# Sums on GpSimd that wait for VectorE's token mix, a cast moved to ScalarE, and wider token mixes of odd batches

## The chip, the core and the metric

The kernel runs on one core of one Trainium2 chip. The metric is the device time of one execution in microseconds, as the median of several executions. The core's engines are TensorE (PE, with its weight loads as PEld), VectorE (DVE), ScalarE (ACT), GpSimd (POOL) and SyncE (SP, which issues most of the DMAs). Each engine takes its own instructions in the order in which the kernel writes them; between engines, semaphores hold an instruction back until its data are there.

## What is computed

Eight batches, each with 8 heads, 576 tokens and a head size of 64. Keys and values are averaged over groups of 8 tokens, so every query meets 72 keys. The attention's result is then the input x (576 x 512 per batch) of a residual MLP block with a token mix:

```python
k_p = k.reshape(B, H, Sp, pool, D).mean(axis=3)          # pool = 8, Sp = 72
v_p = v.reshape(B, H, Sp, pool, D).mean(axis=3)
attn = softmax(scale * q @ k_p.T)                        # per head
x = (attn @ v_p).transpose(0, 2, 1, 3).reshape(B, S, H * D)
tok = np.einsum('ts,bsd->btd', w_tok, alpha1 * x + beta1)
u = x + lam * tok
ch = np.maximum((alpha2 * u + beta2) @ w_ch1, 0.0) @ w_ch2
out = u + lam * ch
```

All inputs and the output are float32; the kernel multiplies in bfloat16 and float16.

## The kernel before

**Blocks.** The tokens are cut into 36 chunks of 128: four per batch, and one more for each pair of batches that holds the last 64 tokens of both. Nine blocks (loop over `n`, L698) take four chunks each through the MLP: 16 first-layer tiles `mlp_A` (four matmuls each into `ps_h`, then a Relu on ScalarE, L547, into `Hj`) and four times four groups `mlp_B` (four matmuls each into `ps_ch`, L565). Beside them, block n carries the attention and the token mix of batch n+1 (`attention(b)`, L665, with b = n+1), so that blocks 0 to 6 do both and blocks 7 and 8 the MLP alone. Batch 0 is done ahead of the loop.

**The order.** Every engine's order is written out by hand. In each block a list `todo` collects pairs of a position and a step; the list is sorted by position (equal ones stay as appended) and carried out in that order (L731). `mlp_A(j)` stands at j, 0 to 15, and the groups of `mlp_B` at 16 to 31; the attention's steps get positions between these. A negative position stands at the head of the block. The order decides only what is ahead of what on each engine; an engine that has nothing to wait for runs ahead into the next block.

**The steps that matter here**, in the order of a batch, with the engine and the line:
- `cast_rem` (L117): the last 64 tokens of q cast, of k summed; GpSimd, three instructions (L121, L123, L124).
- `cast_q` (L128): one half of the heads' q, 128 x 1024 float32, to bfloat16 (L130). GpSimd, for batches 2 to 7.
- `sum_k` (L133): k summed over groups of 8 in three adds (L138 twice, L139), the last into `k_bf`; GpSimd.
- `sum_v_rem` (L430, GpSimd, into `vrem`) and `sum_v` (L411, VectorE, L415 twice and L417, into `v_sum`): the same for v.
- `att_F`, `att_Frem` (L361, L376): transposes of q on TensorE, copied into `qT` by ScalarE (L372, L389).
- `att_K` (L392): TensorE brings the sums of k into `kpT`, copied by VectorE (L407); it also reads `rem_k`.
- `att_V`, `att_Vrem` (L420, L436): the same for v into `vp1`, copied by ScalarE (L427, L443).
- `att_S` (L445): scores of a head in two halves, with an exp on ScalarE each (L454). `att_AV` (L456): five matmuls, then VectorE normalizes into `x` (L474, L476).
- `att_X` (L479): x times lam*alpha1, per pair of heads, into `xs`, the token mix's input; GpSimd for the first three pairs, VectorE for the last.
- `mix_T` (L503): five matmuls of a chunk's token mix into `ps_tok`; VectorE adds x (L513, `u_sb`) and multiplies by alpha2 (L515, `u_bf`, two SBUF inputs).
- `mix_uT` (L518): four transposes of `u_bf` into `ps_uT`, copied by ScalarE into `u_fm` (L528), which is the input of `mlp_A` of the block that the chunk belongs to. An even batch has four of these and an odd one five, since the shared chunk is complete only then.

**Buffers.** q and k of a half batch lie in one of two buffers `qk_raw`, v in one of two `v_u`. `load_qk(b + 1, u)` on SP's queue therefore waits until the cast of q and the sums of k of batch b have read the buffer; loads and output stores share this queue in the written order. The PSUM pool `psA` hands out six banks in turn for everything but `ps_ch`: a new tile waits until the one six before it has been read.

**The start.** `keep_warm` (L64) multiplies a tile `warm` with itself, without use for the result, while the first data are under way; two broadcasts of a row over all partitions (`broadcast`, L263) stand behind it on TensorE. `warm` is filled by one memset (L160).

Of the kernel before, what the change touches and what calls it, by code (L numbers as in the profile page):

```python
# [7 lines left out]
FP = mybir.dt.float32  # L8
# [8 lines left out]
DM = 512  # L17
# [6 lines left out]
def kernel(  # L24
# [18 lines left out]
    nc = tc.nc  # L43
# [3 lines left out]
    const = ctx.enter_context(tc.tile_pool(name="const", bufs=1))  # L47
# [4 lines left out]
    def gp(name):  # L52
        return psA.tile([P, 512], FP, tag="gp", name=name)
# [10 lines left out]
    def keep_warm(count):  # L64

        ps = gp("ps_warm")
        for _ in range(count):
            nc.tensor.matmul(out=ps, lhsT=warm[:, 0:P], rhs=warm)
# [4 lines left out]
    def new_batch(b):  # L73
        st1[b] = {"qT": {}, "ET": [None] * H, "raw": [None] * 2, "q": [None] * 2,
                  "k": [None] * 2, "v": [None] * 2}
# [52 lines left out]
    def cast_q(b, u, copy):  # L128
        bf = work.tile([P, 16, D], BF, tag="q_bf", bufs=3, name="q_bf")
        copy(out=bf, in_=st1[b]["raw"][u][:, 0].rearrange("p e j d -> p (e j) d"))  # L130
        st1[b]["q"][u] = bf

    def sum_k(b, u, eng):  # L133

        t = st1[b]["raw"][u][:, 1]
        bf = work.tile([P, 2, 2, D], BF, tag="k_bf", bufs=4, name="k_bf")
        for n in (4, 2):
            eng.tensor_tensor(out=t[:, :, 0:n], in0=t[:, :, 0:n], in1=t[:, :, n:2 * n], op=ALU.add)  # L138
        eng.tensor_tensor(out=bf, in0=t[:, :, 0:1].to_broadcast((P, 2, 2, D)),  # L139
                          in1=t[:, :, 1:2].to_broadcast((P, 2, 2, D)), op=ALU.add)  # L140
        st1[b]["k"][u] = bf
# [15 lines left out]
    ones_row = const.tile([1, P], FP, tag="ones_row", name="ones_row")  # L157
    nc.vector.memset(ones_row, 1.0)
    warm = const.tile([P, DM], BF, tag="warm", name="warm")
    nc.vector.memset(warm, 0.0)  # L160

    start = const.tile([1, 2], FP, tag="start", name="start")
    nc.gpsimd.memset(start, 0.0)
# [99 lines left out]
    def broadcast(i):  # L263

        ps = psB.tile([P, DM], FP, tag="ch", bufs=2, name="ps_bc")
        nc.tensor.matmul(out=ps, lhsT=ones_row, rhs=vecs[0:1, i])
        return ps
# [152 lines left out]
    def att_V(b, u, copy):  # L420

        ps_v = gp("ps_v")
        nc.tensor.matmul(out=ps_v[:, 0:128], lhsT=sel_main.rearrange("p h e g -> p (h e g)"),
                         rhs=st1[b]["v"][u].rearrange("p r d -> p (r d)"))
        for hh in range(2):
            rows = slice(64 * hh, 64 * hh + 64)
            copy(out=vp1_pool[b % 2][hh][rows, 2 * u:2 * u + 2, 0:64],  # L427
                 in_=ps_v[rows, 0:128].rearrange("p (r d) -> p r d", r=2))
# [7 lines left out]
    def att_Vrem(b, copy):  # L436

        ps_v = gp("ps_v")
        vr = ps_v[:, 0:264].rearrange("p (a x) -> p a x", x=66)
        for a in range(4):  # L440
            nc.tensor.matmul(out=vr[:, a], lhsT=sel_rem[:, a], rhs=vrem_pool[b % 2])
        for hh, rows in ((0, slice(64, 72)), (1, slice(32, 64))):
            copy(out=vp1_pool[b % 2][hh][rows], in_=vr[rows])  # L443
# [35 lines left out]
    def att_X(b, h0, h1, eng=nc.vector):  # L479

        x, xs = st1[b]["x"], xs_pool[b % 2]
        cols = slice(D * h0, D * h1)
        eng.tensor_tensor(  # L483
            out=xs[:, 0:4, cols], in0=x[:, 0:4, cols],
            in1=lamal_bc[:, cols].unsqueeze(1).to_broadcast((P, 4, D * (h1 - h0))), op=ALU.mult)
        p0 = 64 * (b % 2)
        eng.tensor_tensor(out=xs[p0:p0 + 64, 4, cols], in0=x[p0:p0 + 64, 4, cols],
                          in1=lamal_bc[p0:p0 + 64, cols], op=ALU.mult)
# [29 lines left out]
    def mix_uT(key):  # L518
        s = st2[key]
        i = where[key]  # L520
        blk, at = i // 4, i % 4
        if blk not in u_fm:
            u_fm[blk] = work.tile([P, 4, 512], BF, tag="u_fm", bufs=3, name="u_fm")
        ps_uT = gp("ps_uT").bitcast(BF)
        for cc in range(4):
            nc.tensor.transpose(out=ps_uT[0:P, 128 * cc:128 * cc + 128],  # L526
                                in_=s["u_bf"][:, 128 * cc:128 * cc + 128], identity=identity_bf)
        nc.scalar.copy(out=u_fm[blk][:, :, 128 * at:128 * at + 128],  # L528
                       in_=ps_uT[:, 0:512].rearrange("p (c t) -> p c t", t=128))
# [50 lines left out]


    new_batch(1)
    keep_warm(6)
    ps_lam = broadcast(0)
    nc.scalar.copy(out=lam_bc, in_=ps_lam)
    keep_warm(2)
    ps_lamal = broadcast(1)
    nc.scalar.copy(out=lamal_bc, in_=ps_lamal)
    cast_q(0, 0, nc.vector.tensor_copy)
# [71 lines left out]
        mlp_A(0, j, 256, 512)  # L661
    fill_v(1)


    def attention(b):  # L665


        late = b == 1
        todo = [(0.55 if late else -2.0, lambda: cast_rem(b, nc.gpsimd)),
                (10.0 if late else 6.0, lambda: sum_v_rem(b, nc.gpsimd)),  # L670
                (12.4 if late else 7.2, lambda: att_Vrem(b, nc.scalar.copy))]
        for u in range(2):
            copy = nc.scalar.copy if late and u else nc.gpsimd.tensor_copy
            q_at, f_at, k_at, v_at = (((0.5, 3.6, 5.4, 9.5), (6.0, 8.2, 10.0, 11.6))[u] if late else
                                      (-1.0 + 6.6 * u, 2.7 + 6.6 * u, 5.5 + 6.6 * u, 4.2 + 6.6 * u))
            todo.append((q_at, lambda u=u, copy=copy: cast_q(b, u, copy)))
            todo.append((q_at + 0.1, lambda u=u: sum_k(b, u, nc.gpsimd)))
            todo.append((f_at, lambda u=u: att_F(b, u)))
            todo.append((f_at + 0.1, lambda u=u: att_Frem(b, (u,), nc.scalar.copy)))
            todo.append((k_at, lambda u=u: att_K(b, u, nc.vector.tensor_copy)))  # L680
            todo.append((v_at, lambda u=u: sum_v(b, u)))
            todo.append((v_at + 1.6, lambda u=u: att_V(b, u, nc.scalar.copy)))
        for h in range(8):
            at = 13.3 + 1.0 * h if late else 13.1 + 1.0 * h
            todo.append((at, lambda h=h: att_S(b, h)))
            todo.append((at + 2.0, lambda h=h: att_AV(b, h)))
            if h % 2:
                eng = nc.vector if h == 7 else nc.gpsimd
                todo.append((at + 2.1, lambda h=h, eng=eng: att_X(b, h - 1, h + 1, eng)))
        for c in range(5):  # L690
            at = 25.2 + 0.8 * c if late else 24.6 + (0.8 if b % 2 else 1.0) * c
            todo.append((at, lambda c=c: mix_T(b, c)))
            if c < 4 or b % 2:
                key = (b, c) if c < 4 else (b - 1, 4)
                todo.append((at + 1.8, lambda key=key: mix_uT(key)))
        return todo

    for n in range(NBLK):  # L698
        todo = []
        for j in range(0 if n else 4, NJ):  # L700
            todo.append((j, lambda j=j: mlp_A(n, j)))
        for m in range(4):
            for part in range(4):
                at = 16 + (4 * m + part if n else 4 * part + m)
                todo.append((at, lambda m=m, part=part: mlp_B(n, m, part)))
        if n == 0:
            todo.append((12.6, lambda: mix_T(0, 4)))
            todo.append((13.0, lambda: row_of_xs(1, nc.gpsimd)))
            todo.append((9.4, lambda: setup_wtok(4, nc.scalar.copy)))
            todo.append((10.8, lambda: setup_rowsum(4)))  # L710
            todo.append((24.2, setup_wtok_odd))
            for g in range(1, 4):
                todo.append((4 * g - 0.8, lambda g=g: setup_bias(g)))
            for g in range(4):
                todo.append((3.0 + 1.5 * g, lambda g=g: load_w2(g)))
        if n == NBLK - 2:
            for j in range(NJ):
                todo.append((0.5 + 1.5 * j, lambda j=j: scale_w2(j)))
        b = n + 1
        if b < B:  # L720
            todo += attention(b)
            if b + 1 < B:
                new_batch(b + 1)
                for u in range(2):
                    at = 21.0 + 0.2 * u if b == 1 else 0.4 + 1.0 * u
                    todo.append((at, lambda b=b, u=u: load_qk(b + 1, u)))
                    at = 23.0 + 0.2 * u if b == 1 else 5.8 + 6.6 * u
                    todo.append((at, lambda b=b, u=u: load_v(b + 1, u)))
                todo.append((21.1 if b == 1 else 0.9, lambda b=b: load_rem(b + 1)))
                todo.append((23.1 if b == 1 else 6.0, lambda b=b: load_v_rem(b + 1)))  # L730
        for _, do in sorted(todo, key=lambda x: x[0]):  # L731
            do()
# [30 lines left out]
```

The softmax here doesn't subtract the row's maximum and nothing guards it: scores larger than these inputs give would overflow.

## Time and profile before

| what | value |
|---|---|
| median of 10 runs | 372.12 us (371.08 to 372.55) |
| the profiled execution | 372.23 us, of which the span from first to last instruction is 370.4 us |
| mean granted TensorE clock | 0.995 |
| VectorE busy | 216.6 us, 58% of the span |
| ScalarE busy | 202.2 us, 55% |
| GpSimd busy | 146.2 us, 39% |
| chain that ended last: TensorE | 86% of the span; `ps_h` 32%, `ps_ch` 31%, `ps_tok` 11% |
| DMA | 43.27 MB, mean 117 GB/s |

A row of the profile names the engine, the line of the kernel, the operation and its tiles (out <- in). "Idle before" is the time that the engine stood still ahead of an instruction, with the instruction that released it. A row of stretches gives, for each engine, its busy time and number of instructions in that stretch, then the granted clock, the share of the DMA engines and the bandwidth. Matmuls overlap in the pipeline, so the time that one takes on TensorE is read from start to start (0.216 us for 512 columns), not from its duration (0.38 us); and some matmul records are missing, which shows as a gap of one matmul.

### The profile page before, as it was taken

The page shows a single profiled execution, that of the slowest core. Times are in us where ns is not written, and L with a number is a line of the kernel's source. Part 1 is how long each engine was busy: PE and PEld are TensorE (multiplying, and loading weights), DVE is VectorE, ACT ScalarE, POOL GpSimd, SP SyncE. Part 2 cuts the span into 40 slices and gives each one's busy share as a digit, 9 for nine tenths or more (in the row PEclk, how much of TensorE's full clock was granted, in tenths as well). Part 3 has the DMA queues.
Part 4 walks back from the last instruction along what each step waited for, and adds up shares of the span by engine and source line. Part 5 has one row for each costly group of instructions (what it writes and reads, how often), then busy time and mean ns, then how long its engine had stood idle before and what let it go on. Part 6 is the DMA issues. An engine that isn't in the chain of part 4 may idle for free.

```text
span 370.4 us, 6111 instructions
## 1 busy us (share of the span) xinstructions
PE 357.0 (96%) x2308; PEld 196.5 (53%) x2350; DVE 216.6 (58%) x427; ACT 202.2 (55%) x408; POOL 146.2 (39%) x188
## 2 busy tenths in 40 slices
PE   8789999999999999899999998999999999999995
PEld 2467655455545554455455554555455545544544
DVE  7775645972795369724974389427953687643011
ACT  2865984279415960498129922695159704812810
POOL 7866918800692049402870179006930410000000
PEclk9989999999999999999999999999999999999999
DMA  7999993058014910192108302570010002002002
GB/s 246 258 227 324 242 290 123 26 193 278 28 41 143 288 28 32 56 320 65 58 28 286 128 31 58 157 255 30 28 57 2 28 31 58 2 28 85 2 28 85
DMA packets 19575, 43.27 MB, mean 117 GB/s; under 512 B 2193, under 2 KB 4565, under 8 KB 19546
## 3 DMA queue, kind: packets, MB, share of 16 engines
q1 hardware_dynamic: 17488, 37.89, 30.6%
q0 software_dynamic: 1888, 4.86, 6.9%
q8 instruction: 18, 0.29, 0.3%
q10 hardware_dynamic: 170, 0.14, 0.1%
q14 instruction: 11, 0.09, 0.1%
HBM read 38.30 MB, written 9.44 MB: 129 GB/s over the span
## 4 chain that ended last, share of the span: by engine, by line
PE 86%; DVE 5%; ACT 2%; DMA 2%; POOL 2%; issue 1%; SPq 1%; POOLq 0%; DVEq 0%
PE ps_h L542 32%; PE ps_ch L565 31%; PE ps_tok L511 11%; PE ps_sc L452 4%; DMA rem_v_raw<-in_v_dram 2%; PE ps_av L469 2%; DVE u_bf L515 2%; PE ps_uT L526 2%; PE ps_q L368 2%; DVE u_sb L513 1%; SPq L84 1%; ACT Hj L547 1%; POOL v_u L415 1%; DVE xs L483 1%; PE ps_av L472 0%
## 5 line engine op out<-in xcount | busy, mean ns | idle before, releaser
L542 PE MATMUL ps_h<-u_fm,w 128*128 128x512 bf16 (+1 forms) x574 | 133.6, 373 | 1.4 <-ACT u_fm L528 0.4
L565 PE MATMUL ps_ch<-w,Hj 128*128 128x512 bf16 x496 | 124.3, 379 | 1.0 <-issue 0.2
L547 ACT ACTIVATE Hj<-ps_h,bias_cols 128x512 bf16<-128x512 f32 x144 | 96.7, 691 | 39.0 <-PE ps_h L542 37.9
L542 PEld LDWEIGHTS <-w 128*128 128x128 bf16 x592 | 64.8, 114 | 47.9 <-issue 0.6
L483 POOL TENSOR_TENSOR xs<-x_tm,lamal_bc 128x512 bf16<-128x512 f32 x24 | 30.5, 1271 | 136.7 <-DVE x_tm L476 136.7
L565 PEld LDWEIGHTS <-Hj 128*128 128x128 bf16 x592 | 56.1, 98 | 51.6 <-issue 0.2
L528 ACT COPY u_fm<-ps_uT 128x512 bf16<-128x512 bf16 x36 | 21.0, 586 | 87.9 <-PE ps_uT L526 87.8
L454 ACT ACTIVATE ET<-ps_sc 128x288 f16<-128x288 f32 (+1 forms) x128 | 51.7, 489 | 12.2 <-PE ps_sc L452 11.8
L511 PE MATMUL ps_tok<-xs,wtT 128*128 128x512 bf16 (+1 forms) x194 | 49.0, 379 | 0.7 <-PE ps_vec L277 0.2
L407 DVE CAST kpT<-ps_kp 64x288 bf16<-64x288 f32 x31 | 14.1, 455 | 51.5 <-PE ps_kp L403 51.2
L572 DVE TENSOR_TENSOR u_sb<-u_sb,ps_ch 128x512 f32<-128x512 f32 (+1 forms) x37 | 24.9, 673 | 24.9 <-PE ps_ch L565 23.8
L571 DVE TENSOR_TENSOR ps_ch<-lam_bc,ps_ch 128x512 f32<-128x512 f32 x32 | 22.1, 691 | 24.8 <-PE ps_ch L565 24.7
L515 DVE TENSOR_TENSOR u_bf<-u_sb,al_bc 128x512 bf16<-128x512 f32 (+1 forms) x39 | 35.2, 902 | 1.4
L138 POOL TENSOR_TENSOR qk_raw<-qk_raw 128x512 f32<-128x512 f32 (+1 forms) x28 | 33.0, 1177 | 1.1
L476 DVE TENSOR_TENSOR x_tm<-ps_av,rec 128x320 f32<-128x320 f32 x64 | 31.5, 491 | 2.7
L513 DVE TENSOR_TENSOR u_sb<-x_tm,ps_tok 128x512 f32<-128x512 f32 (+1 forms) x40 | 27.3, 682 | 7.7 <-PE ps_tok L511 7.1
L474 DVE RECIPROCAL rec<-ps_av 128x5 f32<-128x5 f32 x64 | 12.4, 193 | 31.8 <-PE ps_av L472 31.5
L511 PEld LDWEIGHTS <-wtT 128*128 128x128 bf16 (+1 forms) x200 | 18.3, 98 | 21.5 <-DVE xs L483 2.6
L452 PE MATMUL ps_sc<-qT,kpT 128*128 128x288 bf16 (+1 forms) x128 | 27.9, 299 | 1.1 <-ACT qT L389 0.8
L469 PEld LDWEIGHTS <-ET 72*128 72x128 f16 (+1 forms) x256 | 16.7, 100 | 14.2 <-DVE vp L427 0.5
L469 PE MATMUL ps_av<-vp,ET 72*128 72x66 f16 (+1 forms) x256 | 18.8, 196 | 0.4 <-DVE vp L427 0.4
L415 DVE TENSOR_TENSOR v_u<-v_u 128x512 f32<-128x512 f32 (+1 forms) x30 | 18.4, 613 | 0.8
(113 smaller groups left out, 307.2 us busy)
## 6 DMA issues: line engine op xcount, KB each, us to landing
qk_raw<-in_q_dram SPq DMA_DIRECT2D x16, 512.0 KB, 7.4
qk_raw<-in_k_dram SPq DMA_DIRECT2D x16, 512.0 KB, 7.9
v_u<-in_v_dram SPq DMA_DIRECT2D x32, 256.0 KB, 7.7
out_dram<-u_sb SPq DMA_DIRECT2D x32, 256.0 KB, 2.3
w<-in_moe_w_ch_dram POOLq DMA_DIRECT2D x2, 1024.0 KB, 13.6
w<-in_moe_w_ch_dram POOLq DMA_DIRECT2D x4, 512.0 KB, 10.7
rem_raw<-in_q_dram SPq DMA_DIRECT2D x8, 128.0 KB, 6.2
rem_raw<-in_k_dram SPq DMA_DIRECT2D x8, 128.0 KB, 5.4
```

Source lines behind the costliest of these rows:

```text
L138: eng.tensor_tensor(out=t[:, :, 0:n], in0=t[:, :, 0:n], in1=t[:, :, n:2 * n], op=ALU.add)
L452: nc.tensor.matmul(out=ps_sc[0:n, 0:288], lhsT=kpT_pool[u][:, j, r, 72 * hh:72 * hh + n], rhs=st["qT"][u][:, h % 4, :])
L454: nc.scalar.activation(out=ET[0:n, 64 + j:64 + S + j:2], in_=ps_sc[0:n, 0:288], func=AF.Exp, bias=0.0, scale=1.0 / 64)
L469: nc.tensor.matmul(out=av[:, c, :], lhsT=ET[:, m0:m0 + 256:2], rhs=vp1)
L476: nc.vector.tensor_tensor(out=x[:, :, dd:dd + D], in0=av[:, :, 0:64], in1=rec.unsqueeze(2).to_broadcast((P, 5, D)), op=ALU.mult)
L483: eng.tensor_tensor(out=xs[:, 0:4, cols], in0=x[:, 0:4, cols], in1=lamal_bc[:, cols].unsqueeze(1).to_broadcast((P, 4, D * (h1 - h0))), op= ...
L511: nc.tensor.matmul(out=ps_tok, lhsT=wtT[0:kk, at, t0:t0 + P], rhs=xs[0:kk, sc, :], start=(sc == 0), stop=(sc == 4))
L513: nc.vector.tensor_tensor(out=s["u"][p0:p1, :], in0=st1[b]["x"][p0:p1, c, :], in1=ps_tok[p0:p1, 0:DM], op=ALU.add)
L515: eng.tensor_tensor(out=s["u_bf"][p0:p1, :], in0=s["u"][p0:p1, :], in1=al2_bc[p0:p1, :], op=ALU.mult)
L542: nc.tensor.matmul(out=ps_h[:, t0:t1], lhsT=w1_of(cc, j), rhs=u_fm[n][:, cc, t0:t1], start=(cc == 0), stop=(cc == 3))
L547: nc.scalar.activation(out=t, in_=ps_h, func=AF.Relu, bias=bias_cols[:, j:j + 1], scale=1.0)
L565: nc.tensor.matmul(out=ps, lhsT=Hj[n, j][:, 128 * m:128 * m + 128], rhs=w2_of(n, j, cols), start=(j == 0), stop=(j == NJ - 1))
```

## The change

Four things change. First, for batches 2 to 7, GpSimd's work on the next batch (`cast_rem`, `sum_k`, `sum_v_rem`) starts with a tiny copy, `pool_wait`, that reads a word which VectorE writes in `tick`; the tick stands at position 29.4 of the block before, behind the last `mix_T`. Both halves of `sum_k` then follow one another at the head of the block. Second, for the same batches `cast_q` is done by ScalarE at 28.7 and 30.2 of the block before, in place of GpSimd at -1.0 and 5.6. Third, positions move: `att_Vrem` from 7.2 to 11.6, `att_V` from 5.8 and 12.4 to 7.6 and 13.2, the token mixes of odd batches from 0.8 to 0.9 apart, and each `mix_uT` from 1.8 to 2.2 behind its `mix_T` (in all batches of the loop; batch 1 keeps its other positions). Fourth, at the start, `warm` is filled with four nonzero values in turn by four memsets of every fourth column, and of the eight warm-up matmuls around the broadcasts four are left.

```diff
-    nc.vector.memset(warm, 0.0)
+    for i, x in enumerate((1.37, -0.73, 0.59, -1.91)):
+        nc.vector.memset(warm[:, i:DM:4], x)
...
-    keep_warm(6)
+    keep_warm(4)
     ps_lam = broadcast(0)
     nc.scalar.copy(out=lam_bc, in_=ps_lam)
-    keep_warm(2)
     ps_lamal = broadcast(1)
...
+    ticks = const.tile([1, 2], FP, tag="ticks", name="ticks")
+
+    def tick():
+        nc.vector.memset(ticks[:, 0:1], 0.0)
+
+    def pool_wait():
+
+        nc.gpsimd.tensor_copy(out=ticks[:, 1:2], in_=ticks[:, 0:1])
...
-                (12.4 if late else 7.2, lambda: att_Vrem(b, nc.scalar.copy))]
+                (12.4 if late else 11.6, lambda: att_Vrem(b, nc.scalar.copy))]
...
-                                      (-1.0 + 6.6 * u, 2.7 + 6.6 * u, 5.5 + 6.6 * u, 4.2 + 6.6 * u))
-            todo.append((q_at, lambda u=u, copy=copy: cast_q(b, u, copy)))
-            todo.append((q_at + 0.1, lambda u=u: sum_k(b, u, nc.gpsimd)))
+                                      (None, 2.7 + 6.6 * u, 5.5 + 6.6 * u, 4.2 + 6.6 * u))
+            k_from = q_at + 0.1 if late else -1.0 + u
+            if late:
+                todo.append((q_at, lambda u=u, copy=copy: cast_q(b, u, copy)))
+            todo.append((k_from, lambda u=u: sum_k(b, u, nc.gpsimd)))
...
-            todo.append((v_at + 1.6, lambda u=u: att_V(b, u, nc.scalar.copy)))
+            todo.append((v_at + (1.6 if late else 3.4 - u), lambda u=u: att_V(b, u, nc.scalar.copy)))
...
+        todo.append((29.4, tick))
+        if b > 1:
+            todo.append((-2.1, pool_wait))
         for c in range(5):
-            at = 25.2 + 0.8 * c if late else 24.6 + (0.8 if b % 2 else 1.0) * c
+            at = 25.2 + 0.8 * c if late else 24.6 + (0.9 if b % 2 else 1.0) * c
             todo.append((at, lambda c=c: mix_T(b, c)))
             if c < 4 or b % 2:
                 key = (b, c) if c < 4 else (b - 1, 4)
-                todo.append((at + 1.8, lambda key=key: mix_uT(key)))
+                todo.append((at + 2.2, lambda key=key: mix_uT(key)))
...
                 for u in range(2):
+                    todo.append((28.7 + 1.5 * u, lambda b=b, u=u: cast_q(b + 1, u, nc.scalar.copy)))
```

`late` is true for batch 1 alone.

## The prediction

> **What bounds it now.** The page's first row comes first, then the stretches by block, then the waits of TensorE, then the timeline of the places that the waits name. A "block" is one pass of the loop over n; block n works on batch n+1, and a position is the number by which its todo list is sorted (0 to 32; one position between two whole numbers is one group of four matmuls).
>
> ```profile
> PE 357.0 (96%) x2308; PEld 196.5 (53%) x2350; DVE 216.6 (58%) x427; ACT 202.2 (55%) x408; POOL 146.2 (39%) x188
> ```
>
> TensorE is busy nearly throughout, and 86% of the chain that ended last is TensorE, so time is gained only where TensorE stands still. Three blocks side by side:
>
> ```profile
> 154.40:193.28 38.88, 38.56 (x252) 21.09 (x255) 24.14 (x46) 22.30 (x46) 17.64 (x20) 1.00 0.36 119
> 193.28:233.44 40.16, 38.94 (x255) 21.22 (x259) 24.92 (x46) 22.90 (x47) 17.71 (x20) 1.00 0.35 116
> ...
> 272.31:311.32 39.01, 38.75 (x255) 21.24 (x259) 23.03 (x46) 22.79 (x47) 5.17 (x6) 1.00 0.09 28
> ```
>
> Batches 4, 5 and 7. An odd batch has four transposes more than an even one (4 x 0.055 us, by the start-to-start time in the timeline: 0.22). Batch 5 is 1.28 longer than batch 4; batch 7, odd too, is 0.13 longer. The column that differs is GpSimd's: 17.7 us busy against 5.2, since behind batch 7 there is no next batch to sum. So batch 7 is this trace's own trial of a mix stage without GpSimd.
>
> ```profile
> PEld L526 <- DVE u_bf L515: 4.4, 6, 1.0
> PEld L511 <- DVE xs L483: 2.6, 6, 0.5
> PE ps_uT L526 <- DVE u_bf L515: 2.1, 5, 0.6
> ```
>
> The few waits that TensorE has are on `u_bf`, VectorE's product for the transposes, and on `xs`. In batch 3, then in batch 7:
>
> ```profile
> 146.26 1.48 DVE L515 TENSOR_TENSOR u_bf<-u_sb,al_bc 128x512 bf16<-128x512 f32 x1
> 147.16 2.53 POOL L138 TENSOR_TENSOR qk_raw<-qk_raw 128x512 f32<-128x512 f32 x2
> ...
> 149.71 0.69 DVE L515 TENSOR_TENSOR u_bf<-u_sb,al_bc 128x512 bf16<-128x512 f32 x1
> 149.77 1.22 POOL L139 TENSOR_TENSOR k_bf<-qk_raw 128x256 bf16<-128x256 f32 x1
> ...
> 151.16 1.06 DVE L515 TENSOR_TENSOR u_bf<-u_sb,al_bc 64x512 bf16<-64x512 f32 x1
> 152.28 0.40 PE L526 MATMUL ps_uT<-identity_bf,u_bf 128*128 128x128 bf16 x4 [0.56 <-DVE u_bf L515]
> ```
>
> ```profile
> 308.45 0.69 DVE L515 TENSOR_TENSOR u_bf<-u_sb,al_bc 64x512 bf16<-64x512 f32 x1
> 309.19 0.40 PE L526 MATMUL ps_uT<-identity_bf,u_bf 128*128 128x128 bf16 x4
> ```
>
> L515 reads two SBUF tiles. It takes 0.69 alone and 1.48 or 1.06 where a GpSimd sum runs; two transposes then arrive late, and by the starts of the matmuls around them TensorE loses 0.57 + 0.72 = 1.29 us (single missing records, gaps of 0.22 each, set aside). In batch 7 it loses 0.13. Even batches have spacing enough for `u_bf`, but L483 on VectorE (0.93 beside GpSimd in batch 4, 0.72 in batch 7) holds back their first token mix: 0.22.
>
> **The change, part by part.**
>
> *The wait of GpSimd and q's cast (gain).* The tick follows the fifth token mix in VectorE's order (29.4 after 28.2 to 28.6), so none of cast_rem, sum_k or sum_v_rem can meet L483 or L515. Tick and copy cost 0.06 and 0.10 (rows of the smallest memsets, L82 and L613). In odd batches, spacing 0.9 and a transpose 2.2 behind its mix also put one more group of `ps_ch` matmuls (0.86) ahead of the last transpose, which covers batch 7's 0.13. Gains: batches 3 and 5, 1.29 each = 2.58; batch 7, 0.13; even batches, 3 x 0.22 = 0.66; batch 1, whose last transpose stays between the same two groups, about 0.15 of its 0.3, as L515 there falls from 1.05 to 0.69 but follows other VectorE work. Sum **-3.5**, bounds -2.7 and -3.7.
>
> A rule of the Trainium skill bears on this: SBUF, section "Who interferes with whom", has it that a VectorE instruction with two SBUF inputs and a GpSimd instruction that reads SBUF exclude each other, the later one waiting for all of the earlier. The rows agree (0.69 becomes 1.48; L571, with one input in PSUM, keeps 0.69). But the rule also speaks against the change: sums moved out of the mix meet the next two-input work, sum_v (L415, 1.15 for two, then 0.29), which VectorE starts 1.5 us into the block. By the rule alone, each of its three steps may wait for a whole GpSimd step (1.27), and so 3.8 would be lost again per block, 23 in six. By the rows sum_v has cover: its matmul, att_V, is moved from 5.8 to 7.6, that is 7.6 us into the block, and 1.5 + 1.44 + 3.8 = 6.7. I take nothing for it.
>
> *GpSimd's new due times.* Behind the waiting copy stand all its sums, then the xs products (due 19 us in, far away); behind the sums on SP's queue stand the loads of the next q, k and v, which need their buffers, and behind those the output stores. In blocks 2 to 6 VectorE is through the fifth mix about 1.4 (even) to 1.9 us before the block ends. From -1.2: cast_rem 0.40 + 0.47 + 0.45, to +0.2; sum_k(0), 2.08 + 0.74 alone (L138, L139), with VectorE's 1.44 in between: +4.5; att_K(0) asks for it at +5.7. sum_k(1), the same again: +8.7, asked for at +12.4; sum_v_rem, 1.25 + 0.31: +10.3, asked for at +11.5, where att_Vrem now stands. Covered by 1.2. The loads go out at +4.5 and +8.7, land in 8 us (DMA issues), and are needed at +33: nothing, with 16 us of cover; the stores come later.
> In block 1 the tick stands behind VectorE's evacuations of block 0, which end about where block 1 begins: GpSimd starts 1.5 us later against the block than above, so k(0) is ready at +5.9 against +5.7, sum_v_rem at +11.8 against +11.5. I take **+0.5**, ends 0 and +1.0.
>
> *ScalarE's new order (loss).* The casts of q, 1.04 each (the one L130 row on ScalarE), fall into the mix, where ScalarE only copies transposes (0.59 each) and waits 1.6 before each: hidden. The batch 2 data have landed by then, since its loads are issued at 37 to 44 us and land in some 13, and the cast comes near 72. But att_Vrem's copies (0.75) move from 7.2 to 11.6, and att_V(1)'s (0.52) from before the first scores to behind them, into the stretch where ScalarE is fullest:
>
> ```profile
> 127.39 0.52 ACT L427 CAST vp<-ps_v 64x128 f16<-64x128 f32 x2
> 127.94 0.69 ACT L547 ACTIVATE Hj<-ps_h,bias_cols 128x512 bf16<-128x512 f32 x1
> 128.52 0.82 ACT L454 ACTIVATE ET<-ps_sc 72x288 f16<-72x288 f32 x2
> 129.19 0.68 ACT L547 ACTIVATE Hj<-ps_h,bias_cols 128x512 bf16<-128x512 f32 x1
> 129.75 0.84 ACT L454 ACTIVATE ET<-ps_sc 128x288 f16<-128x288 f32 x2
> ```
>
> There ScalarE runs back to back: 0.57 for a Relu, 0.67 for a pair of exps, 0.55 for the two copies. Replayed with the moved copies, it starts the Relu of j = 13 at 127.84, as early as before (the copies that left earlier places let it catch up, then it pays them), the first exps at 128.42, the copies of V at 129.10, the Relu of j = 14 at 129.65 where it had been 129.19; that ends at 130.33 in place of 129.87. Its PSUM tile is, six tiles later in the ring of psA, that of the second half of S(2), which TensorE starts at 130.15. So 0.28 of slack becomes a wait of some **0.25 per batch, six batches: +1.5**. No row shows this wait; the ends are 0 (the replay is 0.2 off, or the copies slip in) and 0.5 (the whole 0.46 lands on TensorE and S(3) adds to it): 0 to +3.0. I take the replay's own value.
>
> *The start.* Four strided memsets for one: the row of L160 has 0.27, that of a 128-column memset (L188) 0.17, so between 0.7 and 1.1 for 0.27. VectorE idles 0.91 before L261 for a DMA, which hides it. TensorE starts warm-up at 1.8 instead of 1.3, and drops four matmuls of 0.43: the second broadcast comes about 1.3 earlier. Yet the heads start when VectorE has k(0,1), which waits for its DMA (L138, 11.99) and then runs to v_sum at 17.0: **0**. Here too a rule is to be weighed: TensorE: Matmul & The Clock Gate, "Part 1", says that some 3.4 us of sustained matmuls release the half-rate clock. By it the warm-up would have done its work by 9 us, and cutting it risks half-rate transposes. The row says otherwise:
>
> ```profile
> 12.41 1.06 PE L368 MATMUL ps_q<-identity_bf,q_bf 128*128 128x128 bf16 x8
> 15.03 1.12 PE L452 MATMUL ps_sc<-qT,kpT 128*72 128x288 bf16 x4
> ```
>
> Eight transposes in 1.06 us at 12.4, after ten busy us; the same eight take 0.61 in later blocks. So multiplying zeros did not release the clock (full rate comes near 15.7), and cutting it can cost little; the new data are not zero and may release it sooner. Granted clock 0.50 stands in the stretch 19 to 22.6 us; if it moves, half of 3.5 busy us is at stake, most of it behind ScalarE's copies of wtT. Ends -0.7 and +0.7.
>
> **The sum.** -3.5 + 0.5 + 1.5 + 0 = -1.5. The profiled execution took 372.23 us, its span of 370.4 and 1.8 around it, against a median of 372.12; 372.12 - 1.5 = **370.6 us**.
>
> **Rivals.** (1) *The moved copies are hidden*: no TensorE wait in S. For it: 0.28 of slack was there and the replay overruns it only a little. Then -3.5 + 0.5 = -3.0: 369.1. (2) *The relief doesn't come*: two-input work and GpSimd meet elsewhere on the path, or the late transposes wait on VectorE's own queue. Against it stands batch 7. Then gains of 1 to 2 us are eaten by the 1.5 and 0.5: about 372.1. (3) *Slower, by k's sum*: att_K(0) at 5.5 stands in TensorE's order and waits for `k_bf`, in every block, because GpSimd now begins after the mix instead of 11 us before the block. It decides from +5.7 on; my +4.5 has 1.2 of cover. If tick, semaphores and lock make it +6.6, six waits of 0.9 are +5.4: 372.12 - 1.5 + 5.4 = 376.0; a wait of 0.25 (+5.95) cancels the gain, and a middling case, 0.5 late, gives 370.6 + 3.0 = 373.6. For it: the wait is new and all sums stand behind it; against it: the durations are rows.
>
> **Chances.** Forecast 0.45, rival 1 0.22, rival 2 0.14, rival 3 0.19. What a measurement of this kernel tells from no change is about 0.2%, 0.75 us. Forecast and its bounds are faster than that in nine of ten, rival 1 always: 0.62 faster; 0.18 the same (rival 2 and the weak edge of the forecast); 0.20 slower. The range leaves out half of rival 3 and the best of rival 1: 368.7 to 373.4; the forecast's own is 369.4 to 371.8.
>
> **What would show it.** Right: L515 at 0.69 in every mix stage and no wait of L526 on it; odd blocks near 39; the GpSimd sums in the first ten us of a block; L454's tiles making TensorE wait near position 15. Wrong: waits of L400 on GpSimd's k_bf or of L441 on vrem in blocks 2 to 6; L415 stretched past 4 us with L423 waiting; ScalarE's casts with transposes' copies late behind them; another granted clock between 10 and 25 us.

## The result: 369.82 us

The changed kernel takes 369.82 us in the median (369.44 to 370.18, 9 runs), against 372.04 for the kernel before in the same comparison (371.08 to 372.89, 32 runs): a ratio of 0.9942, 95% interval 0.9933 to 0.9951. Beside two of the later experiments, on one chip with them, it took 370.44, ratio 0.9956 (0.9940 to 0.9972). Forecast were 370.6, range 368.7 to 373.4.

Two rows of the page of the changed kernel, whose span is 368.3 us: the busy time of the engines, and the group of `u_bf` on VectorE. The added lines move the numbers of lines: L516 is what L515 was, L543 the first layer, L566 the second, L527 the transposes.

```profile
PE 355.8 (97%) x2304; PEld 196.2 (53%) x2346; DVE 219.3 (60%) x437; ACT 213.6 (58%) x420; POOL 126.6 (34%) x182
...
L516 DVE TENSOR_TENSOR u_bf<-u_sb,al_bc 128x512 bf16<-128x512 f32 (+1 forms) x39 | 27.3, 700 | 1.4
```

The mean of `u_bf` has fallen from 902 to 700 ns: the product is no longer lengthened in any mix. ScalarE has 11 us more to do (213.6 against 202.2) and GpSimd 20 less. The stretches of the batches shown before, 4, 5 and 7, each from the first matmul of `ps_h` of its block to the next:

```profile
152.68:191.65 38.97, 38.67 (x252) 21.12 (x255) 24.78 (x47) 24.94 (x50) 13.98 (x19) 1.00 0.33 119
191.65:230.84 39.19, 38.90 (x255) 21.34 (x259) 25.07 (x47) 24.16 (x49) 14.58 (x21) 1.00 0.35 119
269.81:309.00 39.19, 38.90 (x255) 21.33 (x259) 25.09 (x47) 23.04 (x48) 13.19 (x16) 1.00 0.09 28
```

The odd blocks are down from 40.17 to 39.19, and batch 7 is now just like batch 5, so what set them apart is gone. But the even block went from 38.88 to 38.97 and batch 7 from 39.01 to 39.19: something new costs time in every block. The waits no longer list `u_bf` for the transposes; new is GpSimd's wait, of up to 14.7 us, which no one waits for:

```profile
POOL ticks L671 <- DVE ticks L667: 73.4, 6, 14.7
...
PEld L512 <- DVE xs L484: 1.9, 6, 0.3
```

In batch 3 the last product of the mix ends at 151.04, and the last transposes start at 151.60 without a wait; GpSimd's copy follows the tick, and its sums follow the copy:

```profile
150.35 0.69 DVE L516 TENSOR_TENSOR u_bf<-u_sb,al_bc 64x512 bf16<-64x512 f32 x1
...
151.21 0.18 POOL L671 COPY ticks<-ticks 1x1 f32<-1x1 f32 x1 [11.70 <-DVE ticks L667]
...
151.60 0.39 PE L527 MATMUL ps_uT<-identity_bf,u_bf 128*128 128x128 bf16 x4
```

And here is the new cost, first ScalarE and then TensorE in block 2, positions 11.6 to 16:

```profile
126.04 0.75 ACT L444 CAST vp<-ps_v 8x264 f16<-8x264 f32 x2
126.81 1.27 ACT L548 ACTIVATE Hj<-ps_h,bias_cols 128x512 bf16<-128x512 f32 x2
127.97 0.82 ACT L455 ACTIVATE ET<-ps_sc 72x288 f16<-72x288 f32 x2
128.64 0.51 ACT L428 CAST vp<-ps_v 64x128 f16<-64x128 f32 x2
129.18 0.69 ACT L548 ACTIVATE Hj<-ps_h,bias_cols 128x512 bf16<-128x512 f32 x1
```

```profile
127.06 0.41 PE L453 MATMUL ps_sc<-qT,kpT 128*72 128x288 bf16 x2
127.30 0.22 PE L424 MATMUL ps_v<-v_sum,sel_main 128*128 128x128 f16 x1
127.55 1.02 PE L543 MATMUL ps_h<-u_fm,w 128*128 128x512 bf16 x4
...
129.67 0.53 PE L453 MATMUL ps_sc<-qT,kpT 128*72 128x288 bf16 x2
130.04 1.02 PE L566 MATMUL ps_ch<-w,Hj 128*128 128x512 bf16 x4
```

`att_V`'s matmul (127.30) keeps TensorE for 0.05 us from start to start, yet the first-layer tile of j = 14 starts only at 127.55, 0.20 late: its PSUM bank is that of j = 12, whose Relu stood behind the two copies of `att_Vrem` (126.04) and ended at 127.50. The second half of S(2) starts 0.25 after the first (129.67, from the length of the two together and the start of 130.04 behind them) where 0.12 is usual: its bank is that of j = 14, whose Relu stood behind the copies of `att_V(1)` (128.64) and ended at 129.87. Together 0.33 per block, the same in all six. In the kernel before, the tile of j = 14 starts without this delay and the two halves are 0.13 apart.

So the account of the two profiles: the span fell by 2.16 us, 0.44 of it ahead of the loop (first matmul of `ps_h` at 30.55 against 30.99), 1.72 within it.

### The profile page after: what moved, and what is told of

Its sections match the earlier page's. It is cut to its first block, busy times and chain, and to the rows that moved or that the text cites. A ratio compares the mean times of both kernels' runs of the same rounds, so it can differ in the third digit from the quotient of the medians.

```text
span 368.3 us, 6142 instructions
## 1 busy us (share of the span) xinstructions
PE 355.8 (97%) x2304; PEld 196.2 (53%) x2346; DVE 219.3 (60%) x437; ACT 213.6 (58%) x420; POOL 126.6 (34%) x182
## 4 chain that ended last, share of the span: by engine, by line
PE 90%; ACT 3%; DVE 2%; DMA 2%; issue 1%; SPq 1%; ACTq 0%
PE ps_ch L566 33%; PE ps_h L543 32%; PE ps_tok L512 12%; PE ps_sc L453 4%; PE ps_uT L527 2%; PE ps_av L470 2%; DMA qk_raw<-in_k_dram 2%; ACT Hj L548 2%; PE ps_q L369 1%; SPq L84 1%; PE ps_kp L401 1%; DVE x_tm L477 1%; DVE qk_raw L138 1%; PE ps_av L473 1%; ACT qT L373 0%
## 5 line engine op out<-in xcount | busy, mean ns | idle before, releaser
L543 PE MATMUL ps_h<-u_fm,w 128*128 128x512 bf16 (+1 forms) x575 | 133.7, 373 | 1.4 <-ACT u_fm L529 0.4
L566 PE MATMUL ps_ch<-w,Hj 128*128 128x512 bf16 x489 | 123.9, 379 | 1.3 <-issue 0.2
L543 PEld LDWEIGHTS <-w 128*128 128x128 bf16 x592 | 64.1, 114 | 48.2 <-issue 0.6
L566 PEld LDWEIGHTS <-Hj 128*128 128x128 bf16 x592 | 55.5, 98 | 49.2 <-issue 0.2
L453 PE MATMUL ps_sc<-qT,kpT 128*128 128x288 bf16 (+1 forms) x128 | 29.3, 306 | 0.9 <-DVE kpT L408 0.8
L138 POOL TENSOR_TENSOR qk_raw<-qk_raw 128x512 f32<-128x512 f32 (+1 forms) x28 | 29.7, 1059 | 1.1
L516 DVE TENSOR_TENSOR u_bf<-u_sb,al_bc 128x512 bf16<-128x512 f32 (+1 forms) x39 | 27.3, 700 | 1.4
L671 POOL COPY ticks<-ticks 1x1 f32<-1x1 f32 x6 | 1.1, 177 | 73.4 <-DVE ticks L667 73.4
L416 DVE TENSOR_TENSOR v_u<-v_u 128x512 f32<-128x512 f32 (+1 forms) x30 | 23.4, 780 | 0.8
```

The lines of the kernel that those rows point to most:

```text
L453: nc.tensor.matmul(out=ps_sc[0:n, 0:288], lhsT=kpT_pool[u][:, j, r, 72 * hh:72 * hh + n], rhs=st["qT"][u][:, h % 4, :])
L516: eng.tensor_tensor(out=s["u_bf"][p0:p1, :], in0=s["u"][p0:p1, :], in1=al2_bc[p0:p1, :], op=ALU.mult)
L543: nc.tensor.matmul(out=ps_h[:, t0:t1], lhsT=w1_of(cc, j), rhs=u_fm[n][:, cc, t0:t1], start=(cc == 0), stop=(cc == 3))
L566: nc.tensor.matmul(out=ps, lhsT=Hj[n, j][:, 128 * m:128 * m + 128], rhs=w2_of(n, j, cols), start=(j == 0), stop=(j == NJ - 1))
```

## The experiments

"Loop" is the time from the first matmul of `ps_h` to the end of the span in the profile; it repeats to within 0.03 us where blocks are alike (337.74 and 337.76 for the changed kernel in two executions), while the part ahead of it does not. Blocks are those of batches 4 and 5. All ratios are to the kernel before on the same chip.

| kernel | median us | ratio, 95% interval | even block | odd block | loop |
|---|---|---|---|---|---|
| before | 372.04 | | 38.87 | 40.17 | 339.46 |
| changed | 369.82 | 0.9942 (0.9933 to 0.9951) | 38.97 | 39.19 | 337.74 |
| changed, again | 370.44 | 0.9956 (0.9940 to 0.9972) | 38.97 | 39.19 | 337.76 |
| V(1)'s copies on VectorE | 369.04 | 0.9918 (0.9903 to 0.9933) | 38.85 | 39.08 | 337.03 |
| Vrem's copies on VectorE | 369.17 | 0.9921 (0.9906 to 0.9937) | 38.85 | 39.07 | 336.99 |
| both on VectorE | 368.00 | 0.9889 (0.9869 to 0.9909) | 38.66 | 38.87 | 335.88 |
| both, again | 367.87 | 0.9893 (0.9875 to 0.9911) | 38.66 | 38.87 | 335.87 |
| changed, GpSimd doesn't wait | 370.48 | 0.9954 (0.9943 to 0.9966) | 39.18 | 39.19 | 338.34 |
| changed, old spacing | 370.54 | 0.9963 (0.9949 to 0.9977) | 38.97 | 39.32 | 338.19 |
| before, new spacing alone | 369.78 | 0.9937 (0.9923 to 0.9951) | 38.87 | 39.30 | 337.57 |
| changed, old start | 369.88 | 0.9941 (0.9929 to 0.9953) | 38.96 | 39.18 | 337.69 |
| changed, tick at 31.6 | 376.07 | 1.0103 (1.0085 to 1.0121) | 39.80 | 40.02 | 344.05 |
| changed, q cast by GpSimd | 370.69 | 0.9958 (0.9943 to 0.9973) | 38.97 | 39.19 | 338.19 |

**What makes TensorE wait in the scores?** Two theories: ScalarE is late by the moved copies, or the moved matmul shifts the ring of PSUM tiles. Giving the copies to VectorE leaves the ring as it is.

```diff
+            v_copy = nc.vector.tensor_copy if u and not late else nc.scalar.copy
-            todo.append((v_at + (1.6 if late else 3.4 - u), lambda u=u: att_V(b, u, nc.scalar.copy)))
+            todo.append((v_at + (1.6 if late else 3.4 - u), lambda u=u, v_copy=v_copy: att_V(b, u, v_copy)))
```

> The changed kernel, with the two copies of att_V(1) (batches 2 to 7) done by VectorE instead of ScalarE; positions and the order of the PSUM tiles stay. Theory (ScalarE is late by the moved copies, so that tiles come back late): the two gaps near position 14 and 15, 0.20 + 0.13 us per block in the profile of the changed kernel, become one of 0.20 at most and the second is gone; 369.8 - 6 x 0.13 = 369.0, and 367.9 if both go. Rival (the place of att_V's tile in the ring of PSUM tiles is what makes TensorE wait, whoever copies): both gaps stay and the time is 369.8.

369.04 us; the gap of 0.13 is gone and the one of 0.19 stands, as the first branch of the theory had it.

```diff
-                (12.4 if late else 11.6, lambda: att_Vrem(b, nc.scalar.copy))]
+                (12.4 if late else 11.6, lambda: att_Vrem(b, nc.scalar.copy if late else nc.vector.tensor_copy))]
```

> The changed kernel with the copies of att_Vrem alone done by VectorE; att_V(1) stays with ScalarE. Theory: att_Vrem's 0.75 us makes the Relu of j = 12 late, which holds back the tile of j = 14 (0.20 per block), and leaves its trace in the later gap too, since ScalarE runs without a pause from there: both gaps shrink, the first goes, 0 to 0.13 stays of the second: 368.0 to 368.7. Rival (the copy of V behind the first exps is what matters): the first gap stays at 0.2.

369.17 us, beyond the expected 368.7: the gap at j = 14 is gone, but the one in S(2) grew from 0.13 to 0.20. TensorE reached S(2) earlier by what it had no longer lost, and met the same late Relu. So either edit alone takes 0.12 off a block. With both edits:

> The changed kernel with the copies of att_V(1) and of att_Vrem (batches 2 to 7) done by VectorE, positions unchanged. Theory (ScalarE's lateness alone makes the waits near positions 13 to 15): both gaps are gone, even blocks 38.65 to 38.7 us, odd ones 38.9, 6 x 0.31 less than the changed kernel: 367.7 to 368.2. Rival (VectorE's new copies delay its own work on kpT or on the sums of v, and TensorE waits there instead): a gap moves to the matmuls that read kpT, blocks at 38.9 and more, 368.8 or above.

368.00 us and both gaps gone. ScalarE, then VectorE, in block 2 of that kernel:

```profile
126.72 0.69 ACT L548 ACTIVATE Hj<-ps_h,bias_cols 128x512 bf16<-128x512 f32 x1 [0.24 <-PE ps_h L543]
127.73 0.69 ACT L548 ACTIVATE Hj<-ps_h,bias_cols 128x512 bf16<-128x512 f32 x1 [0.32 <-PE ps_h L543]
128.31 0.81 ACT L455 ACTIVATE ET<-ps_sc 72x288 f16<-72x288 f32 x2
128.98 0.67 ACT L548 ACTIVATE Hj<-ps_h,bias_cols 128x512 bf16<-128x512 f32 x1
129.53 0.83 ACT L455 ACTIVATE ET<-ps_sc 128x288 f16<-128x288 f32 x2
```

```profile
125.85 0.87 DVE L444 CAST vp<-ps_v 8x264 f16<-8x264 f32 x2 [3.25 <-PE ps_v L442]
126.85 0.92 DVE L408 CAST kpT<-ps_kp 64x288 bf16<-64x288 f32 x2
128.03 0.59 DVE L428 CAST vp<-ps_v 64x128 f16<-64x128 f32 x2 [0.26 <-PE ps_v L424]
```

ScalarE now pauses ahead of two Relus (0.24 and 0.32, waiting for TensorE), and VectorE takes the copies in 0.87 and 0.59 us, where it had 3.25 us of idle time. Even blocks are at 38.66 and odd ones at 38.87, apart by just the four transposes. Beside the changed kernel on one chip:

> The changed kernel with the copies of att_V(1) and att_Vrem on VectorE once more, beside the changed kernel: 6 x 0.31 = 1.9 us less than it, 367.9, if the profile's blocks speak for the medians; a difference under 1 us would say that other parts give back what the blocks gain.

The changed kernel's own expectation in that comparison:

> The changed kernel itself, beside the next two on one chip: 369.8, ratio 0.994.

367.87 against 370.44, for which 369.8 had been expected. The loops differ by 1.89, as expected; the rest of the medians' 2.6 lies ahead of the loop or within the intervals. This version is the fastest of all that ran, 1.1% below the kernel before.

**Is it the wait or the spacing that cures the odd blocks?** Four corners: neither (the kernel before), both (the change), and each alone. First, the change without the wait:

```diff
-        if b > 1:
-            todo.append((-2.1, pool_wait))
```

> The changed kernel without the copy that makes GpSimd wait for the tick; the sums run ahead into the mix again, the wider spacing and ScalarE's casts stay. Theory (the wait brings the gain): VectorE's products for the transposes are back at 1.0 to 1.5 us, xs costs 0.22 per block again, odd blocks lose 0.3 to 0.7 more: 370.8 to 372.0. Rival (the spacing alone would have done it): products are long but no transpose waits, only xs does: at most 6 x 0.1 to 0.2, 370.0 to 370.9 with odd blocks as even ones plus 0.2.

370.48 us. The odd block is as good as with the wait. In the timeline of batch 3 an early product is long beside GpSimd's sum, but by the end of the mix the sums are through (there are no casts among them) and the last product takes 0.69; no transpose is late:

```profile
143.86 1.10 DVE L516 TENSOR_TENSOR u_bf<-u_sb,al_bc 128x512 bf16<-128x512 f32 x1
144.37 2.86 POOL L138 TENSOR_TENSOR qk_raw<-qk_raw 128x512 f32<-128x512 f32 x2
...
150.14 0.69 DVE L516 TENSOR_TENSOR u_bf<-u_sb,al_bc 64x512 bf16<-64x512 f32 x1
150.30 0.39 PE L527 MATMUL ps_uT<-identity_bf,u_bf 128*128 128x128 bf16 x4
```

Only even blocks lose: 0.21 each, TensorE's wait for `xs`, as the theory had it. The rival was right on the transposes and the time; its odd blocks, even ones plus 0.2, did not come (39.19 beside 39.18). Then the spacing by itself, on the kernel before:

```diff
-            at = 25.2 + 0.8 * c if late else 24.6 + (0.8 if b % 2 else 1.0) * c
+            at = 25.2 + 0.8 * c if late else 24.6 + (0.9 if b % 2 else 1.0) * c
...
-                todo.append((at + 1.8, lambda key=key: mix_uT(key)))
+                todo.append((at + 2.2, lambda key=key: mix_uT(key)))
```

> The kernel before, with the spacing of the change alone (token mixes of odd batches 0.9 apart, transposes 2.2 behind their mix). Theory: a part of the 1.29 us per odd block goes, since one more group of ps_ch matmuls stands ahead of the last transposes, but the products stay long beside GpSimd: blocks of batches 3 and 5 fall from 40.2 to 39.4 to 39.8, and the time to 370.7 to 371.6. Rival (spacing does it all): odd blocks at 39.1 and 369.7 or less. Rival (spacing does nothing while GpSimd is in the way): 372.0.

369.78 us, as fast as the whole change; its loop is 0.17 shorter. So all else in the change is worth nothing on balance: on top of the spacing it saves 0.44 in two odd blocks, 0.21 in three even ones and 0.23 in the first, together 1.7, and pays 1.9 in the scores. Both the odd block (39.30) and the time came out better than the theory's 39.4 and 370.7, near the rival by which spacing does it all. The product stays long, yet only the last transposes are late, by 0.44:

```profile
149.69 1.58 POOL L433 TENSOR_TENSOR rem_v_raw<-rem_v_raw 64x256 f32<-64x256 f32 x2
149.91 1.06 DVE L515 TENSOR_TENSOR u_bf<-u_sb,al_bc 64x512 bf16<-64x512 f32 x1
...
151.02 0.40 PE L526 MATMUL ps_uT<-identity_bf,u_bf 128*128 128x128 bf16 x4 [0.27 <-DVE u_bf L515]
```

The reverse, the change with the old spacing:

```diff
-            at = 25.2 + 0.8 * c if late else 24.6 + (0.9 if b % 2 else 1.0) * c
+            at = 25.2 + 0.8 * c if late else 24.6 + (0.8 if b % 2 else 1.0) * c
...
-                todo.append((at + 2.2, lambda key=key: mix_uT(key)))
+                todo.append((at + 1.8, lambda key=key: mix_uT(key)))
```

> The changed kernel with the spacing of the kernel before (token mixes of odd batches 0.8 apart, transposes 1.8 behind): the wait without the spacing. Theory of the prediction (the wait takes 1.16 of the 1.29 us of an odd block, the spacing only the 0.13 of batch 7): odd blocks 39.19 + 0.13 = 39.32, even ones 38.97 as in the changed kernel, 370.2. Rival (the wait is worth what it showed on top of the spacing, 0.44 per odd block): odd blocks at 40.0, 371.4 or more.

370.54 us and odd blocks at 39.32, to the hundredth what the prediction's reading gave; the product is short, and the last transposes come 0.13 after the matmuls ahead of them have gone through:

```profile
150.30 0.69 DVE L516 TENSOR_TENSOR u_bf<-u_sb,al_bc 64x512 bf16<-64x512 f32 x1
151.04 0.40 PE L527 MATMUL ps_uT<-identity_bf,u_bf 128*128 128x128 bf16 x4
```

With the 0.3 us of the scores taken out, an odd block loses 1.29 with neither, 0.44 with the spacing, 0.13 with the wait and nothing with both: the spacing alone cures two thirds of the loss, the wait nine tenths, and the two overlap.

The corner of the wait has more in it than the wait, since q's casts are off GpSimd there too. The run without the wait shows that this counts: its third and fifth products in batch 3 take 0.84 and 0.69, where the kernel before, and the kernel before with the new spacing, have 1.48 and 1.06. What the casts' move and the new order of the sums would do alone, at the old spacing, was not run.

**How much cover has GpSimd's late start?**

```diff
-        todo.append((29.4, tick))
+        todo.append((31.6, tick))
```

> The changed kernel with the tick at 31.6 instead of 29.4, behind the last evacuation of a block, so that GpSimd starts some 3.1 us later (2.6 in the first such block). Theory (k's sum is ready 2.6 us before TensorE asks for it in blocks 2 to 6 and 0.7 in block 1; L400's matmuls wait from there on): waits of 0.5 to 1.2 us in five blocks and of 1.9 to 2.4 in block 1: 374 to 378. Rival (there is more cover, since the sums run faster outside the mix): below 371.

376.07 us. Blocks 2 to 6 are 0.83 longer and block 1 is 2.16 longer (41.13 against 38.97), both inside what was expected. The wait is where the third rival put it:

```profile
PEld L401 <- POOL k_bf L139: 7.2, 6, 1.5
...
PE ps_kp L401 <- POOL k_bf L139: 4.4, 6, 1.0
```

**What does ScalarE's cast buy?** The cast goes back to GpSimd, behind the wait.

```diff
-            if late:
-                todo.append((q_at, lambda u=u, copy=copy: cast_q(b, u, copy)))
+            if not late:
+                q_at = -1.1 + u
+            todo.append((q_at, lambda u=u, copy=copy: cast_q(b, u, copy)))
...
-                    todo.append((28.7 + 1.5 * u, lambda b=b, u=u: cast_q(b + 1, u, nc.scalar.copy)))
```

> The changed kernel with the casts of q back on GpSimd, behind its wait (order: rem, cast and sums of half 0, cast and sums of half 1). Theory (GpSimd has 2.6 us of cover in blocks 2 to 6, so a cast of 1.03 fits there; in block 1 it has 0.7, and TensorE waits 0.3 to 0.5): 370.1 to 370.4. Rival (ScalarE's casts are what the wait needs): half a us or more in every block, 372 and above. Rival (the casts on ScalarE delay its copies): faster than the changed kernel, below 369.5.

370.69 us, a little over the expected 370.4. The blocks, which the start's scatter doesn't touch, say more: block 1 alone is longer, by 0.41 (39.38), and all others are unchanged. So with the wait in place ScalarE's casts save 0.4 us once. In block 1 the transposes of q wait for the cast:

```profile
PEld L369 <- POOL q_bf L130: 0.6, 1, 0.6
...
PEld L401 <- POOL k_bf L139: 0.4, 1, 0.4
```

**The start.** The old warm-up in the changed kernel:

```diff
-    for i, x in enumerate((1.37, -0.73, 0.59, -1.91)):
-        nc.vector.memset(warm[:, i:DM:4], x)
+    nc.vector.memset(warm, 0.0)
...
-    keep_warm(4)
+    keep_warm(6)
     ps_lam = broadcast(0)
     nc.scalar.copy(out=lam_bc, in_=ps_lam)
+    keep_warm(2)
```

> The changed kernel with the start of the kernel before: one memset of zeros, six and two warm-up matmuls. Theory (the shorter warm-up brings the first block 0.44 us forward, as the two profiles show it): 370.2, with the loop's first matmul back near 31.0 us. Rival (that shift is the phase of the granted clock, different in each execution): 369.8, and the first matmul anywhere from 30.5 to 31.

369.88 us, no change; the first matmul of the loop stands at 30.41. Over all 13 profiles it stands at 30.99, 29.74 and 30.41 with the old start, and between 29.96 and 31.41 with the new one. The start's 0.44 us in the two profiles is scatter.

## Why the prediction was right, and where it was not

**The bound and the gain: right.** TensorE's standing still was the only time to be had. The two losses per odd block (1.29) and the 0.22 for `xs` in even blocks are gone: 40.18 - 1.29 + 0.31 = 39.20, measured 39.19; 38.88 - 0.22 + 0.31 = 38.97, as measured. Block 0 (batch 1) fell by 0.23, against 0.15 taken; it falls as far without the wait (43.96 us) and not at all by the spacing alone (44.20, as before), so there the casts' move and the new order of the sums are enough, beside the new spacing.

**What brought it: half wrong.** The prediction gave the wait all of the 1.29 but the 0.13 that it read from batch 7 and gave to the spacing. As a statement on the wait, with the casts moved, that is confirmed (39.32). As a division of the gain it is not: the spacing alone takes 0.87 of the 1.29, since one more group of matmuls (0.86) ahead of the last transposes covers a long product as well as a short one. The fault lies in calling the 0.86 us a cover for 0.13, when the row beside it said that the product was late by 0.57 and 0.72. The gain came out right because either of the two would have brought most of it.

**GpSimd's due times: right in blocks 2 to 6, too dear in block 1.** In blocks 2 to 6 no matmul waits for the sums, as forecast; k(0) is ready at +3.2 to +3.3, not +4.5. In block 1 it was forecast 0.2 late; GpSimd's copy and the end of the sum in that block, which begins at 74.52:

```profile
74.91 0.18 POOL L671 COPY ticks<-ticks 1x1 f32<-1x1 f32 x1 [14.65 <-DVE ticks L667]
...
78.81 0.79 POOL L139 TENSOR_TENSOR k_bf<-qk_raw 128x256 bf16<-128x256 f32 x1
```

It ends 5.1 us into the block, not 5.9, ahead of the +5.7 at which it is asked for, so the 0.5 us term was nothing. The tick ran 0.24 into the block, about as assumed, but the sums were dearer in the working than on the chip: sum_k(0) was charged 2.82 + 1.44 and took 3.27. VectorE waited too: its sums of v took 2.35 beside it (77.40 to 79.75), not 1.44. That is the lock of the Trainium skill's page SBUF — State Buffer, "Who interferes with whom", seen from the other side: the mean of L415 (L416 now) rose from 613 to 780 ns, and the 7.6 us of cover of its matmul held. The late tick shows where the cover ends: in blocks 2 to 6 k's sum was ready 2.5 us before +5.74, when TensorE asks for it. With the late tick GpSimd starts 3.1 us later, takes 0.17 longer, and 0.06 passes between its end and the matmul; less the 2.5, that is the measured 0.83.

**ScalarE's copies: the mechanism right, the size 0.25 against 0.31.** The mis-sized term is this one. Its working is loose: 130.33 against 130.15 is a wait of 0.18, and it becomes 0.25 only with the 0.05 to 0.06 us between a Relu's end and the matmul that waited for it (127.50 and 127.55 above), which it doesn't name. The replay found the late tile in S(2), and missed the earlier one: j = 14 waits for the bank of j = 12, which the same replay has only after `att_Vrem`'s copies. It compared one pair of the ring where every pair in the crowded stretch had to be compared. 6 x 0.31 = 1.9 instead of 1.5. Rival 1, that the copies are hidden, fell with it, though the median lies about as near to its 369.1 as to 370.6.

**The start: right at 0, with one reading too wide.** The memsets took the upper end (warm-up at 2.19 instead of 1.8) and this stayed hidden. But that multiplying zeros does not release the clock was read from one profile. In two of the three profiles with the old start it was released, near 4.1 us (the kernel before with the new spacing) and 4.7 us (the changed kernel with the old start), for 3.4 us each, and then half rate came back. In the first of them, eight transposes at full rate and the next eight at half rate again:

```profile
6.66 0.62 PE L368 MATMUL ps_q<-identity_bf,q_bf 128*128 128x128 bf16 x8
...
11.09 1.06 PE L368 MATMUL ps_q<-identity_bf,q_bf 128*128 128x128 bf16 x8
```

By the Trainium skill's page TensorE: Matmul & The Clock Gate, Part 1, some 3.4 us of sustained matmuls release the clock, which fits these two: 2.8 and 3.4 us after the first warm-up matmul. It doesn't fit the kernel before, nor the ten profiles with the new start, where the transposes near 12 us all run at half rate. In the changed kernel, ten us after the first warm-up and with TensorE idle for less than 1 us at a time in between:

```profile
12.06 1.06 PE L369 MATMUL ps_q<-identity_bf,q_bf 128*128 128x128 bf16 x8
```

So the early full rate was seen only with the longer warm-up, and the medians show no gain from it (369.88 with the old start). Whether the length of the warm-up or its data decides was not tried.

**The sum in the loop** is then -2.6 (batches 3 and 5) - 0.13 (batch 7) - 0.66 (even) - 0.23 (batch 1) + 1.9 = -1.7, measured -1.72; forecast -1.5. That these two are so near is partly luck: the 0.5 charged for block 1 was not needed, and the 0.36 missing in the scores makes up for most of it. The median moved by 2.2, or 1.6 in the second comparison; the rest lies in the start's scatter and the intervals. Why the start scatters stays open: the clock's part in it was seen, not tried.

## What to carry to other kernels

When two parts of a change cure the same stall, an account that is right in sum may be wrong in its shares: run each part alone. Here two changed numbers, the spacing alone, were as fast as the whole change. In a ring of buffers, a step moved into an engine's busiest stretch is paid by whichever unrelated tile comes one turn of the ring later, so compare every pair there, and give the moved step to an engine that idles at that time. A wait that keeps two engines apart is free only while its cover lasts; 2.2 positions more turned a gain of 0.6% into a loss of 1.0%.

## What the runs showed of the hardware

The time ahead of the loop spread by 1.7 us over executions, while blocks repeated to 0.03. The half rate of TensorE ended at different times. Five transposes of 128 columns take 0.72 to 0.74 us in the kernel before while its column of the granted clock shows 0.50 (19.1 to 22.5 us), and 0.44 behind that. In the changed kernel's first profile, then in its second:

```profile
20.84 0.45 PE L288 MATMUL ps_w<-identity_bf,wt_bf 128*128 128x128 bf16 x5
```

```profile
21.37 0.72 PE L288 MATMUL ps_w<-identity_bf,wt_bf 128*128 128x128 bf16 x5
23.23 0.74 PE L288 MATMUL ps_w<-identity_bf,wt_bf 128*128 128x128 bf16 x5
```

Full rate came near 20.8 us in the one and after 23.2 in the other, and their loops began at 30.55 and 31.41. The column of the granted clock shows 1.00 throughout this time in both, for it shows 1.00 up to the first change that a profile records; so for this part the spacing of equal matmuls tells the rate, and the column doesn't.

In the other profiles the start of the loop goes with the last return to full rate: from 21.1 us with the loop at 29.74 to 23.7 with it at 31.33, nearly in the same order. The first profile above (20.8 and 30.55) is the one that stands apart, and no run changed the clock alone, so this is not shown to be the cause.
